# The last product of a fused attention and feed-forward kernel, its 128-row matmuls cut into two of 64 rows

## The chip, the core and the metric

The kernel runs on one NeuronCore of a Trainium2 chip. The metric is device time in microseconds (us) of one execution. TensorE multiplies: it holds a stationary block (the "weights" of one matmul) of up to 128 rows by 128 columns and streams a moving block of up to 512 columns past it; the sums over the rows go to PSUM, which has eight banks of 512 float32 for each of 128 partitions. VectorE (DVE) and ScalarE (ACT) empty the banks into SBUF, and DMA queues carry data between SBUF and the main memory. In profiles the loading of a stationary block stands on a row of its own, PEld.

## The reference

```python
attn = softmax(mask(q @ k.T / sqrt(64))) @ v          # 2 batches, 12 heads, 448 tokens, head size 64
x = attn as (896, 768)
h = max(x @ w1, x @ w2, x @ w3)                       # 768 -> 768
y = h @ w_out                                         # 768 -> 768
t = y @ w_in2                                         # 768 -> 2048
g = t if t > 0 else exp(t) - 1
out = g @ w_out2                                      # 2048 -> 768
```

The five weight matrices come as float64, everything else as float32.

## The kernel before

All products are computed transposed: a result block has 128 features on the partitions and the 448 tokens of one batch in the free dimension, so it fills most of one PSUM bank. The order of the program is attention (with some of the first product woven into it), then h, y, g and out, one block of 128 output features after another. In the code the results in PSUM are called `ph`, `py`, `pg` and `po`.

To keep float32 accuracy each operand is cut in two numbers of a shorter type (`F32R`): `hi` is the value rounded, `lo` the rest. A product needs three matmuls for each 128 rows of the contraction: hi by hi, hi by the rest of the activations, and lo by hi. `products` (lines 184 to 192) issues them for both batches: four matmuls with the weights `hi` (lines 189 and 190) and two with `lo` (line 192) for one chunk of 128 rows. Every matmul brings its own load of the 128x128 stationary block.

The weights are made by `weight_steps` (lines 144 to 178): a DMA brings float64 words, five DVE steps (lines 158 to 168) turn them into float32, ACT rounds them to `hi` (line 175), and DVE subtracts to get `lo` (line 142). The pool `wp` has two buffers for the raw words and for the float32, and three each for `hi` and `lo`, so this work runs ahead of TensorE by up to three blocks of weights.

The last product stands in lines 541 to 556: for each of the six blocks `f` of 128 output features the 16 chunks of the contraction come in three blocks of weights (6, 5 and 5 chunks), 96 matmuls for both batches together, 576 in all six. `psum` (line 486) gives the banks out in turn, all eight of them. After the 16 chunks DVE copies the bank of batch 0 and ACT that of batch 1 (line 555) into the tile `ot`, and SP's queue writes each to memory (line 556). In the last block of weights of the last `f` the batches are done one after the other, so that only batch 1 is left to copy and write at the very end.

In attention, the scores `s` (line 280) contract over a head size of 64: the two heads of a pair lie in the two row halves of TensorE and write to different banks. Their operands are plain float32; the chip runs such a matmul as two passes, and the profile shows each pass as an instruction of its own. Line 327 transposes `pr` into `pt` through the full array in one pass, and line 350 (`o`) uses all 128 rows and 64 columns.

Of the kernel before, what the change touches and what calls it, by code (L numbers as in the profile page):

```python
# [14 lines left out]
ALU = mybir.AluOpType  # L15
PSUM = bass.MemoryType.PSUM

B, H, S, D = 2, 12, 448, 64
# [7 lines left out]
NF = 2048 // 128  # L26
# [93 lines left out]
def fused_kernel(ctx: ExitStack, tc: tile.TileContext, qk, v, w1, w2, w3, wo, wi2, wo2, outT):  # L120
    nc = tc.nc
# [58 lines left out]
    def load_w(src, n, name):  # L180
        *_, parts = weight_steps(src, n, name)
        return parts

    def products(ps_list, hi, lo, xs_list, c0, n, total):

        for c in range(n):
            cc = c0 + c
            for ps, xs in zip(ps_list, xs_list):
                nc.tensor.matmul(ps, hi[:, c, :], xs[cc][:, 0, :], start=(cc == 0), stop=False)  # L189
                nc.tensor.matmul(ps, hi[:, c, :], xs[cc][:, 1, :], start=False, stop=False)  # L190
            for ps, xs in zip(ps_list, xs_list):
                nc.tensor.matmul(ps, lo[:, c, :], xs[cc][:, 0, :], start=False, stop=(cc == total - 1))  # L192

    x = [[None] * NK for _ in range(B)]
    y = [[None] * NK for _ in range(B)]

    with ExitStack() as s1:
# [13 lines left out]
        with ExitStack() as s2:  # L211
# [236 lines left out]
            def block(k, ready):  # L448

                f, n = AHEAD[k]  # L450
                u = {}

                def product(eng, c):
                    if c == 0:
                        u["ps"] = ps_m.tile([128, S], F32, tag="m", name=f"ph{n}_0_{f}")
                    hi, lo = ahead[f, n]
                    products([u["ps"]], hi[:, c:c + 1], lo[:, c:c + 1], [x[0]], c, 1, NK)

                def keep(eng):
                    if n == 0:  # L460
                        bests[f, 0] = bp.tile([128, S], F32, tag="best0", name=f"best0_{f}")
                    keep_best(bests[f, 0], u["ps"], n)

                t = ready
                for c in range(NK):
                    t = plan.add(product, (c,), {"PE": 610}, k if c == 0 else -20, [t, ready, xs_done[c if k == 0 else NK - 1]],
                        takes=["m"] * (c == 0), mode="x")
                return plan.add(keep, (), {"DVE" if n else "ACT": 540 if n else 420}, 0, [t], gives=["m"])
# [17 lines left out]
        def psum(name):  # L486
            pool, tag = banks[count[0] % 8]
            count[0] += 1
            return pool.tile([128, S], F32, tag=tag, name=name)

        h = [[None] * NK for _ in range(B)]
        for f in range(NK):
            best = [bests.get((f, b)) or bp.tile([128, S], F32, tag=f"best{b}", name=f"best{b}_{f}") for b in range(B)]
            for n, w in enumerate((w1, w2, w3)):
                over = range(1, B) if (f, n) in AHEAD else range(B)
                if (f, n) in AHEAD:
                    hi, lo = ahead[f, n]
                else:

                    with tc.issue_after(last["DVE"].ins):  # L500
                        hi, lo = load_w(w[f], NK, f"w{n}_{f}")
                ps = [psum(f"ph{n}_{b}_{f}") for b in over]
                products(ps, hi, lo, [x[b] for b in over], 0, NK, NK)
                for b in over:
                    keep_best(best[b], ps[b - over[0]], n)
            for b in range(B):
                hs = hp.tile([128, 2, S], F32R, tag="h", name=f"h{b}_{f}")
                nc.scalar.copy(hs[:, 0], best[b])
                sub(nc.vector, hs[:, 1], best[b], hs[:, 0])
                h[b][f] = hs  # L510
        for f in range(NK):
            hi, lo = load_w(wo[f], NK, f"wo_{f}")
            ps = [psum(f"py{b}_{f}") for b in range(B)]
            products(ps, hi, lo, h, 0, NK, NK)
            for b in range(B):
                ys = yp.tile([128, 2, S], F32R, tag="y", name=f"y{b}_{f}")
                nc.scalar.copy(ys[:, 0], ps[b])
                sub(nc.vector, ys[:, 1], ps[b], ys[:, 0])
                y[b][f] = ys
# [3 lines left out]
    g = [[None] * NF for _ in range(B)]  # L523
    for f in range(NF):
        hi, lo = load_w(wi2[f], NK, f"wi2_{f}")
        ps = [psum(f"pg{f}_{b}") for b in range(B)]
# [12 lines left out]
            sub(nc.vector, gs[:, 1], gf, gs[:, 0])  # L539
            g[b][f] = gs  # L540
    for f in range(NK):
        ps = [psum(f"po{f}_{b}") for b in range(B)]
        c0 = 0
        for n in (6, 5, 5):
            hi, lo = load_w(wo2[f, :, c0:c0 + n], n, f"wo2_{f}_{c0}")
            if f == NK - 1 and c0 + n == NF:
                for b in range(B):
                    products([ps[b]], hi, lo, [g[b]], c0, n, NF)
            else:
                products(ps, hi, lo, g, c0, n, NF)  # L550
            c0 += n
        for b in range(B):
            ot = ep.tile([128, S], F32, tag="ot", name=f"ot{f}_{b}")
            rows = outT[128 * f:128 * (f + 1), S * b:S * (b + 1)]
            (nc.scalar.copy if b else nc.vector.tensor_copy)(ot, ps[b])
            nc.sync.dma_start(rows, ot)


# [38 lines left out]
```

## Time and profile before

| | |
|---|---|
| median of 3 runs | 496.99 us (496.43 to 498.34) |
| span of the profiled execution, first to last instruction | 494.9 us |
| what the median has beyond that span | 2.1 us |
| TensorE matmul busy | 488.0 us, 99% of the span |
| TensorE weight loads busy | 425.2 us, 86% |
| VectorE, ScalarE busy | 374.7 us (76%), 183.4 us (37%) |
| the last product, first matmul to last | 374.5 to 491.0 us of the span |

The profile has no time of its own for the profiled execution beside its span. "Busy" counts the time in which at least one instruction of an engine is under way. Matmuls overlap: the duration of one is how long it takes to pass through, and the pace is the distance from one start to the next. "PEclk" is the granted TensorE clock as a share of 2.4 GHz. In a row of the timeline the first number is the start in us from the start of the span, the second the length in us of the (merged) instructions, then follow engine, line, operation, output<-inputs, shapes, and the count; in brackets stands how long the engine was idle ahead of it, and what ended that.

### The profile page before, as it was taken

To read this page: it belongs to the slowest core of one execution; us is meant where nothing else is said; L and a number is where in the kernel's file an instruction comes from. 1 tells how busy PE (TensorE), PEld (TensorE's weight loads), DVE (VectorE), ACT (ScalarE), POOL (GpSimd) and SP (SyncE) were. 2 spreads that over 40 slices of the span, in tenths; PEclk is the share of its full clock that TensorE was granted. 3 is DMA by queue.
4 is the path that set the end of the run, shared out by engine and by line. 5 is a ranking of instruction groups with operands and counts; after the bars stand their busy time and mean duration, and the time that the engine had idled before them with its cause. 6 is when DMAs were issued, how large, how long until landed. Compare 5 with 4: busy or idle time off the path is not lost.

```text
span 494.9 us, 6950 instructions
## 1 busy us (share of the span) xinstructions
PE 488.0 (99%) x2600; PEld 425.2 (86%) x2600; DVE 374.7 (76%) x719; ACT 183.4 (37%) x426; POOL 41.0 (8%) x95
## 2 busy tenths in 40 slices
PE   7999999999999999999999999999999999999997
PEld 3555757899999999999999999999999999999996
DVE  5999995599978778778778888988988756667310
ACT  6999795222202221221223654554553111111100
POOL 4475361000000000000000000000000000000000
PEclk9999999999999999999999999999999999999999
DMA  6635520045433332323332332332332444244010
GB/s 216 229 91 185 212 72 21 1 138 182 142 123 119 127 107 86 130 77 115 127 117 75 127 101 92 128 123 74 102 119 73 138 127 155 93 153 143 2 37 37
DMA packets 13969, 55.88 MB, mean 113 GB/s; under 512 B 1520, under 2 KB 3568, under 8 KB 13936
## 3 DMA queue, kind: packets, MB, share of 16 engines
q1 hardware_dynamic: 13936, 55.45, 33.3%
q8 instruction: 20, 0.33, 0.3%
q14 instruction: 13, 0.11, 0.1%
HBM read 52.69 MB, written 2.75 MB: 112 GB/s over the span
## 4 chain that ended last, share of the span: by engine, by line
PE 94%; DVE 3%; POOL 1%; DMA 1%; ACT 0%; issue 0%; SPq 0%; DVEq 0%; ACTq 0%
PE ph L189 9%; PE ph L192 9%; PE ph L190 9%; PE po L192 8%; PE pg L192 8%; PE po L190 8%; PE pg L190 8%; PE pg L189 8%; PE po L189 8%; PE pt L327 4%; PE o L350 4%; PE s L280 4%; PE py L192 3%; PE py L189 3%; PE py L190 3%; DVE pr L294 1%
## 5 line engine op out<-in xcount | busy, mean ns | idle before, releaser
L189 PE MATMUL ph<-x,hi_w 128*128 128x448 f32 x216 | 79.4, 368 | 0.0
L190 PE MATMUL ph<-x,hi_w 128*128 128x448 f32 x216 | 78.9, 365 | 0.0
L189 PE MATMUL po<-g,hi_wo 128*128 128x448 f32 x192 | 70.2, 366 | 0.0
L189 PE MATMUL pg<-y,hi_wi 128*128 128x448 f32 x192 | 70.2, 366 | 0.0
L190 PE MATMUL pg<-y,hi_wi 128*128 128x448 f32 x192 | 70.2, 365 | 0.0
L190 PE MATMUL po<-g,hi_wo 128*128 128x448 f32 x192 | 70.2, 365 | 0.0
L175 ACT CAST hi_wo<-f_wo 128x768 fp32r<-128x768 f32 (+1 forms) x24 | 18.8, 783 | 125.0 <-PE po L190 56.4
L192 PE MATMUL ph<-x,lo_w 128*128 128x448 f32 x216 | 64.3, 366 | 0.0
L192 PE MATMUL po<-g,lo_wo 128*128 128x448 f32 x192 | 55.4, 366 | 0.0
L192 PE MATMUL pg<-y,lo_wi 128*128 128x448 f32 x192 | 54.6, 365 | 0.0
L142 DVE TENSOR_TENSOR lo_wo<-f_wo,hi_wo 128x768 fp32r<-128x768 f32 (+1 forms) x24 | 21.4, 891 | 31.8 <-ACT hi_wo L175 31.8
L189 PEld LDWEIGHTS ph<-x,hi_w 128*128 128x128 f32 x216 | 40.6, 188 | 3.2
L192 PEld LDWEIGHTS ph<-x,lo_w 128*128 128x128 f32 x216 | 40.6, 188 | 3.2
L190 PEld LDWEIGHTS ph<-x,hi_w 128*128 128x128 f32 x216 | 40.6, 188 | 3.1
L175 ACT CAST hi_w<-f_w 128x768 fp32r<-128x768 f32 x18 | 15.1, 837 | 70.2 <-PE ph L190 45.5
L189 PEld LDWEIGHTS po<-g,hi_wo 128*128 128x128 f32 x192 | 36.1, 188 | 2.8
L189 PEld LDWEIGHTS pg<-y,hi_wi 128*128 128x128 f32 x192 | 36.1, 188 | 2.8
L192 PEld LDWEIGHTS po<-g,lo_wo 128*128 128x128 f32 x192 | 36.1, 188 | 2.8
L192 PEld LDWEIGHTS pg<-y,lo_wi 128*128 128x128 f32 x192 | 36.1, 188 | 2.8
L190 PEld LDWEIGHTS pg<-y,hi_wi 128*128 128x128 f32 x192 | 36.1, 188 | 2.8
L190 PEld LDWEIGHTS po<-g,hi_wo 128*128 128x128 f32 x192 | 36.1, 188 | 2.8
L304 ACT ACTIVATE pr<-pr,nmx 128x384 f32<-128x384 f32 (+1 forms) x72 | 35.9, 502 | 5.3 <-DVE nmx L294 5.3
(80 smaller groups left out, 804.6 us busy)
## 6 DMA issues: line engine op xcount, KB each, us to landing
raw_w<-in_w SPq DMA_DIRECT2D x18, 768.0 KB, 4.4
raw_wi<-in_wi SPq DMA_DIRECT2D x16, 768.0 KB, 4.3
raw_wo<-in_wo SPq DMA_DIRECT2D x12, 768.0 KB, 4.4
raw_wo<-in_wo SPq DMA_DIRECT2D x12, 640.0 KB, 4.0
qk<-in_qk SPq DMA_DIRECT2D x11, 448.0 KB, 4.7
v<-in_v SPq DMA_DIRECT2D x12, 256.0 KB, 3.5
out_t<-ot SPq DMA_DIRECT2D x12, 224.0 KB, 3.1
qk<-in_qk SPq DMA_DIRECT2D x1, 256.0 KB, 3.1
```

Source lines behind the costliest of these rows:

```text
L142: return eng.tensor_tensor(out=out, in0=a, in1=b.bitcast(F32), op=ALU.subtract)
L175: nc.scalar.copy(hi, fb)
L189: nc.tensor.matmul(ps, hi[:, c, :], xs[cc][:, 0, :], start=(cc == 0), stop=False)
L190: nc.tensor.matmul(ps, hi[:, c, :], xs[cc][:, 1, :], start=False, stop=False)
L192: nc.tensor.matmul(ps, lo[:, c, :], xs[cc][:, 0, :], start=False, stop=(cc == total - 1))
L280: nc.tensor.matmul(out, us[e]["qk"][own, 0, C * i:w], us[e]["qk"][own, 1, :w], start=True, stop=True, skip_group_check=True)
L294: nc.vector.tensor_tensor_reduce(out=pr, in0=u["s", g][j or 0][:, at:at + w], in1=mask_r if i == NB else mask[:, FULL - w:], scale=-0.125, ...
L304: nc.scalar.activation(pr, pr, AF.Exp, bias=u["nmx"][:, n:n + 1], scale=-1.0, accum_out=u["l"][:, n:n + 1])
L327: nc.tensor.transpose(pt[:e - C * c, at:at + C], u["pr", j if j is None else j ^ odd, i][:, C * c:e], ident)
L350: nc.tensor.matmul(u["o"][D * j:D * (j + 1), C * c:], u["v"][:, j, c], u["th_r"][:, j ^ odd] if c == NB else u["th"][:, c, j ^ odd, C * c: ...
```

## The change

Each matmul of the last product is cut into one over rows 0 to 63 and one over rows 64 to 127 of the same stationary and moving blocks. The two halves accumulate into banks of their own (so a block `f` holds four banks, not two), and alternate: lower half, upper half, for each of the three terms. When the sums are done, ACT copies the bank of the lower half into `ot`, and DVE adds the bank of the upper half to it, for both batches. Everything ahead of the last product is as it was.

```diff
+    def products_by_rows(pairs, hi, lo, xs_list, c0, n, total):
+
+        for c in range(n):
+            cc = c0 + c
+            for parts in (((hi, 0), (hi, 1)), ((lo, 0),)):
+                for pair, xs in zip(pairs, xs_list):
+                    for w, part in parts:
+                        for ps, at in zip(pair, (0, 64)):
+                            rows = slice(at, at + 64)
+                            nc.tensor.matmul(
+                                ps, w[rows, c, :], xs[cc][rows, part, :], start=cc == 0 and w is hi and part == 0,
+                                stop=cc == total - 1 and w is lo)
...
     for f in range(NK):
-        ps = [psum(f"po{f}_{b}") for b in range(B)]
+        ps = [[psum(f"po{f}_{b}_{r}") for r in range(2)] for b in range(B)]
         c0 = 0
         for n in (6, 5, 5):
             hi, lo = load_w(wo2[f, :, c0:c0 + n], n, f"wo2_{f}_{c0}")
             if f == NK - 1 and c0 + n == NF:
                 for b in range(B):
-                    products([ps[b]], hi, lo, [g[b]], c0, n, NF)
+                    products_by_rows([ps[b]], hi, lo, [g[b]], c0, n, NF)
             else:
-                products(ps, hi, lo, g, c0, n, NF)
+                products_by_rows(ps, hi, lo, g, c0, n, NF)
             c0 += n
         for b in range(B):
             ot = ep.tile([128, S], F32, tag="ot", name=f"ot{f}_{b}")
             rows = outT[128 * f:128 * (f + 1), S * b:S * (b + 1)]
-            (nc.scalar.copy if b else nc.vector.tensor_copy)(ot, ps[b])
+            nc.scalar.copy(ot, ps[b][0])
+            nc.vector.tensor_tensor(out=ot, in0=ps[b][1], in1=ot, op=ALU.add)
             nc.sync.dma_start(rows, ot)
```

On TensorE, at the start of the last product, the row of a matmul names output, moving and stationary block; `po_0` is batch 0 and `po_1` batch 1. Before:

```order
L189 MATMUL po_0_3635<-g_0_2634,hi_wo_0_0_3645 128x448
L190 MATMUL po_0_3635<-g_0_2634,hi_wo_0_0_3645 128x448
L189 MATMUL po_1_3636<-g_1_2642,hi_wo_0_0_3645 128x448
L190 MATMUL po_1_3636<-g_1_2642,hi_wo_0_0_3645 128x448
L192 MATMUL po_0_3635<-g_0_2634,lo_wo_0_0_3646 128x448
L192 MATMUL po_1_3636<-g_1_2642,lo_wo_0_0_3646 128x448
```

With the change, where `po_0_0` and `po_0_1` are the two row halves of batch 0:

```order
L203 MATMUL po_0_0_3635<-g_0_2634,hi_wo_0_0_3647 128x448
L203 MATMUL po_0_1_3636<-g_0_2634,hi_wo_0_0_3647 128x448
L203 MATMUL po_0_0_3635<-g_0_2634,hi_wo_0_0_3647 128x448
L203 MATMUL po_0_1_3636<-g_0_2634,hi_wo_0_0_3647 128x448
L203 MATMUL po_1_0_3637<-g_1_2642,hi_wo_0_0_3647 128x448
L203 MATMUL po_1_1_3638<-g_1_2642,hi_wo_0_0_3647 128x448
```

The order of the terms stays, and each matmul has become a pair; there are 1152 where there were 576.

On DVE, where the first block `f` ends, before:

```order
L168 SCALAR_TENSOR_TENSOR f_wo_2_0_3919<-raw_wo_2_0_3917,f_wo_2_0_3919 128x768
L555 COPY ot_0_3769<-po_0_3635 128x448
L142 TENSOR_TENSOR lo_wo_1_11_3876<-f_wo_1_11_3869,hi_wo_1_11_3875 128x640
L158 TENSOR_SCALAR f_wo_2_6_3967<-raw_wo_2_6_3965 128x640
L160 TENSOR_SCALAR f_wo_2_6_3967<-f_wo_2_6_3967 128x640
```

and with the change:

```order
L168 SCALAR_TENSOR_TENSOR f_wo_2_0_4121<-raw_wo_2_0_4119,f_wo_2_0_4121 128x768
L142 TENSOR_TENSOR lo_wo_1_11_4044<-f_wo_1_11_4037,hi_wo_1_11_4043 128x640
L569 TENSOR_TENSOR ot_0_3867<-po_0_1_3636,ot_0_3867 128x448
L569 TENSOR_TENSOR ot_1_3871<-po_1_1_3638,ot_1_3871 128x448
L158 TENSOR_SCALAR f_wo_2_6_4205<-raw_wo_2_6_4203 128x640
L160 TENSOR_SCALAR f_wo_2_6_4205<-f_wo_2_6_4205 128x640
```

One copy became two additions, and they stand behind the `lo` of the next block's weights rather than ahead of it.

## Rows read from the trace of the kernel before

**Rows 1.** The page: busy time, granted clock, and the chain that ended last
```profile
span 494.9 us, 6950 instructions
PE 488.0 (99%) x2600; PEld 425.2 (86%) x2600; DVE 374.7 (76%) x719; ACT 183.4 (37%) x426; POOL 41.0 (8%) x95
PEclk9999999999999999999999999999999999999999
PE 94%; DVE 3%; POOL 1%; DMA 1%; ACT 0%; issue 0%; SPq 0%; DVEq 0%; ACTq 0%
```

**Rows 2.** Windows over the six blocks of po: busy us (instructions), clock, DMA
```profile
394.00:413.00 19.00, 19.00 (x95) 17.64 (x94) 12.99 (x19) 2.48 (x4) 0.00 (x0) 1.00 0.42 135
...
sum 117.50, PE 116.91 PEld 108.13 DVE 65.22 ACT 17.58 POOL 0.00; mean PE 19.48 PEld 18.02 DVE 10.87 ACT 2.93 POOL 0.00
```

**Rows 3.** The tile po: ns min/median/max of one, first and last start
```profile
L189 PE MATMUL po<-g,hi_wo x192: 361/365/370, 374.5 to 490.6; 128*128 128x448 f32 x192
L192 PE MATMUL po<-g,lo_wo x192: 362/365/370, 375.3 to 491.0; 128*128 128x448 f32 x192
L555 DVE COPY ot<-po x6: 623/624/625, 394.0 to 488.4; 128x448 f32<-128x448 f32 x6
L555 ACT COPY ot<-po x6: 522/527/532, 394.4 to 491.5; 128x448 f32<-128x448 f32 x6
```

**Rows 4.** Timeline within po: matmuls, and the loads for the next ones
```profile
398.83 0.36 PE L189 MATMUL po<-g,hi_wo 128*128 128x448 f32 x1
398.83 0.19 PEld L190 LDWEIGHTS po<-g,hi_wo 128*128 128x128 f32 x1
399.03 0.36 PE L190 MATMUL po<-g,hi_wo 128*128 128x448 f32 x1
```

**Rows 5.** Timeline in attention: scores in the two row halves, two groups of passes
```profile
5.36 1.14 PE L280 MATMUL s<-qk 64*128 64x384 f32 x8 [0.52 <-DMA qk<-in_qk]
60.71 1.17 PEld L280 LDWEIGHTS s<-qk 64*128 64x128 f32 x12 [0.20 <-issue]
60.71 1.57 PE L280 MATMUL s<-qk 64*128 64x384 f32 x12
```

**Rows 6.** Chain that ended last: start us, us, transposes and scores
```profile
58.04 0.80 PE pt L327 x6
70.89 0.92 PE pt L327 x7
```

**Rows 7.** Timeline in attention: F32R matmuls, the last followed by a transpose
```profile
81.12 0.37 PE L190 MATMUL ph<-x,hi_w 128*128 128x448 f32 x1
81.33 0.37 PE L192 MATMUL ph<-x,lo_w 128*128 128x448 f32 x1
81.54 0.27 PE L327 MATMUL pt<-ident,pr 128*128 128x128 f32 x1
```

**Rows 8.** Groups by line and shape: x count, busy us, mean ns of one
```profile
L205 DVE TENSOR_TENSOR best<-ph,best 128x448 f32<-128x448 f32 x24 | 14.0, 619 | 18.9 <-PE ph L192 18.9
L350 PE MATMUL o<-th_r,v 128*64 128x64 f32 x48 | 3.4, 221 | 0.0
```

**Rows 9.** Timeline where the second block f begins, and after
```profile
393.76 0.73 ACT L175 CAST hi_wo<-f_wo 128x640 fp32r<-128x640 f32 x1 [5.35 <-PE po L190]
394.39 0.53 ACT L555 COPY ot<-po 128x448 f32<-128x448 f32 x1
395.38 0.49 DVE L158 TENSOR_SCALAR f_wo<-raw_wo 128x640 int32<-128x640 int32 x1
397.83 0.82 DVE L168 SCALAR_TENSOR_TENSOR f_wo<-raw_wo,f_wo 128x640 int32<-128x640 int32 x1
401.10 0.83 ACT L175 CAST hi_wo<-f_wo 128x768 fp32r<-128x768 f32 x1 [6.18 <-issue]
```

**Rows 10.** Timeline of the end, and four short passes of o
```profile
491.04 0.37 PE L192 MATMUL po<-g,lo_wo 128*128 128x448 f32 x1
491.49 0.53 ACT L555 COPY ot<-po 128x448 f32<-128x448 f32 x1 [18.70 <-PE po L192]
492.05 0.33 SPq L556 DMA_DIRECT2D out_t<-ot  x1
...
59.69 0.28 PE L350 MATMUL o<-th_r,v 128*64 128x64 f32 x4
```

## The prediction

> **What bounds the kernel now.** First the page: TensorE has a matmul under way for 99% of the span, the chain of waits that ended last runs over PE for 94% of it, and the granted clock is full (2.4 GHz) throughout [rows 1]. The reader is to see that only the pace of TensorE, and what stands behind its last matmul, can move the time. Second the windows over the last product, po: TensorE is busy for 116.9 of 117.5 us, DVE for 65.2, ACT for 17.6 [rows 2]. The other engines have room there. Third the pace, which busy time does not give, since matmuls overlap. The first of the 576 matmuls starts at 374.5, the last at 491.0 [rows 3]: 116.5 us over 575 steps is 202.6 ns a step, and single steps in the timeline agree (398.83 to 399.03) [rows 4]. Streaming 448 columns, one in each clock of 2.4 GHz, would take 186.7 ns. So **16 ns in each step are something else**, 9.2 us over the stage. The change is worth what it does to these 16 ns, and costs what it adds.
>
> **The row halves.** The change turns 576 steps into 576 pairs. How long is a pair? The scores in attention are the one place of the trace with two 64-row matmuls in two row halves and two banks. A group of 8 passes (two pairs 384 columns wide, two 128 wide) takes 1.14 us, one of 12 (two more pairs, 256 wide) 1.57 us [rows 5]. So 512 columns more, in both halves, cost 0.43 us. These are plain float32 passes, which take two clocks a column: a seventh transpose of 128 columns adds 0.12 us to six [rows 6], against 107 ns at two clocks. At that rate 512 columns are 427 ns, if the halves run side by side, and 853 ns if one waits for the other. **They run side by side**, loads included, and little is left over: 3 ns in two pairs, with 10 ns of rounding in each of the two rows, at most some 10 ns a pair.
>
> So do the 16 ns go with the halves? The rows allow two readings. Either they belong to changing the stationary block of the full array, and the scores are free of them since they run in halves; or they belong to a stream of the type F32R at one column a clock, and the scores are free of them since their streams run at half that rate. What tells the two apart is the transposes: full array, a new stationary block each, two clocks a column, and the seventh costs 0.11 to 0.12 us where 0.107 is the stream [rows 6]. The full array changes its block there for a few ns. And where an F32R matmul is followed by a transpose, whose load is short and done early, the step is still 0.21 us, as between two F32R matmuls before it (81.12, 81.33, 81.54) [rows 7]. So the 16 ns come with the F32R stream, whatever follows. Each half streams the same 448 columns of F32R at the same rate, beside the other, so I take the pair at today's step, 202.6 ns: **no change from the matmuls, 0.0 us**. The bounds, from these rows: below, a pair as free of extras as the scores, 186.7 + 3 = 189.7 ns, which is 576 x 12.9 ns = -7.4 us; above, two halves that wait for each other, 2 x 186.7 + 3 = 376 ns, +100 us. I take the middle because the transposes, the nearest row for the full array, speak against the first, and the scores against the last.
>
> The Trainium skill says in "TensorE: Matmul & The Clock Gate", Part 3, The mechanism, that a weight load overlaps a matmul in flight only where the row groups differ. By that rule the full array would pay for its loads now and the halves would not, and the sum would be the lower bound. Here the trace differs: in po the load of the next block starts with the running matmul of the full array, both at 398.83 [rows 4].
>
> The number of matmuls doubles: 1152 in 117 us is one in 101 ns. Four short passes of `o` fit in 0.28 us, where one alone takes 0.22 [rows 10, 8], so four start within 0.06 us. Handing out matmuls costs nothing here; if it could only keep 110 ns apart, it would cost 1152 x 9 ns = 10 us.
>
> **The change of tiling.** Going from the full array to halves idles the loads for 0.20 us in attention [rows 5], against nothing in an unbroken run. It happens once: **+0.2 us**.
>
> **Emptying the banks.** For each block f one DVE copy (624 ns) and one ACT copy (527) [rows 3] become two ACT copies and two DVE additions; the same form of addition, a bank and a tile, takes 619 ns in line 205 [rows 8]. Over six blocks ACT gets 3.2 us more and DVE 12 x 0.619 - 6 x 0.624 = 3.7 us more, against 52 us in which DVE is idle and 100 for ACT [rows 2]. The queues: ACT rounds weights until 394.49 and then copies, now twice, to about 395.5; DVE adds at 394.95 and 395.5, and the next block's first weight step, at 395.38 before [rows 9], starts near 396.1, 0.7 us later. Its last step then ends at 399.4 and not 398.65, still ahead of the rounding at 401.10, which waits for a free buffer [rows 9]. The `lo` of the next block now stands ahead of the additions and does not wait. Four banks a block leave the other four of eight to the next block, and they are needed again only 19 us later. Nothing of it reaches TensorE: **0.0 us**. If that cover were gone, each block would pay the 0.7 us, 4 us in all.
>
> **The end.** Now ACT starts the last copy at 491.49, 0.45 us after the start of the last matmul, and the write to memory follows at 492.05 [rows 10]. With the change an addition stands between them: 0.62 us and a hand-over of 0.03, as between that copy's end at 492.02 and the write. All of it is on the path: **+0.65 us**.
>
> **Sum.** 0.0 + 0.2 + 0.65 = +0.85 us. The profiled execution's span, 494.9, becomes 495.7; the median of the runs has 2.1 us more than that span, and I keep those: 496.99 + 0.85 = **497.8 us**. The uncertain part is the step: in one stretch of attention F32R steps take 0.206 to 0.207 us (81.12 to 81.54) [rows 7], 4 ns over po's, and I allow as much on the other side but somewhat less: 200 to 206.5 ns is -1.5 to +2.2 us, so this case has the range 496 to 500.
>
> **The rivals.**
> *The 16 ns vanish in the halves.* The block change of the full array is then what costs, by a mechanism that spares transposes. For it: every F32R matmul of the trace runs in the full array, and every float32 matmul that is no transpose runs in halves or on half the columns, so no row shows F32R in halves. Against it: the transposes and the step of rows 7. Time: 497.8 - 7.4 = 490.4 us. Chance 0.31.
>
> *The pair is longer than the step,* since the second half starts after the first and the next pair waits for both. What the rows leave open is up to some 7 ns a pair [rows 5]; 576 x 7 = 4.0 us, 501.8 us. It decides from 205.4 ns a pair on, where 0.85 + 576 x 2.8 ns reaches 2.5 us. For it: all those steps would pay it, and nothing covers it. Against it: the 512 columns that cost 0.43 us. Chance 0.17.
>
> The Trainium skill's page "TensorE: Matmul & The Clock Gate", Part 3, Measured speedup vs the span model, gives about 4 ns for each further tile. That speaks against this change, and would make an estimated 576 x 4 = 2.3 us of this rival. No row here resolves it.
>
> *The halves do not run side by side in F32R,* so that the change does not do what it says. The scores deliver a sum in each half every two clocks, one a clock for both; F32R would deliver two a clock down the same columns into two banks, and no row shows that rate on all 128 columns. If one a clock is the limit, a pair takes 376 ns and the kernel 497.8 + 100 = 598 us. Chance 0.08.
>
> **How the numbers follow.** My own case has 0.44. About 0.5% (2.5 us) is what a measurement of this kernel can tell from no change. Faster than that needs a pair under 196.8 ns, which the first rival brings: 0.31. Slower needs one over 205.4 ns: the second and third rival, 0.25, and of my own case the top end, 0.02, makes 0.27. Same: 0.42. The range is to leave out at most 0.2: from below the first rival's 490.4, with a ns a pair to spare, to above the second's 501.8, leaving out the third and some of the second's tail: 489.8 to 503.0.
>
> **What would show it.** In the profile after, first and last start of po's matmuls give the pair: 116.7 us between them means 202.6 ns and this forecast, 109 us the first rival, 121 the second, 216 the third. The two matmuls of a pair should start within 10 ns of each other. The last matmul should be followed by an ACT copy, an addition of 0.62 us and the write; TensorE should not idle where a block f begins, and DVE's weight steps should come 0.7 us later there. A stage of another length at an unchanged pair, or an idle TensorE, would make the prediction wrong in its sum as well as in its reason.

## The result, and the profile after

| | before | after |
|---|---|---|
| first comparison | 497.06 us, 4 runs (496.43 to 498.34) | 501.11 us, 4 runs (500.46 to 501.76) |
| ratio, 95% interval | | 1.0077 [1.0060, 1.0095] |
| the same kernel again, on another occasion | 497.03 us, 12 runs (496.73 to 504.93) | 499.96 us, 6 runs (497.99 to 500.72) |
| ratio, 95% interval | | 1.0049 [1.0032, 1.0066] |
| span of the profiled execution, first comparison | 494.9 us | 498.7 us (its own time 500.46) |

The change makes the kernel slower, by 0.8% in the first comparison and by 0.5% in the second: beyond the 0.5% that I called measurable, and at its edge. Its ten executions do not lie around one value: eight lie between 499.8 and 501.8, two at 498.0 and 498.1. The experiments show two lengths of one step on TensorE behind this, both at full granted clock; the text calls them the short and the long step.

The page of the kernel after, its busy times, its chain and its costliest group:

```profile
span 498.7 us, 8124 instructions
PE 490.9 (98%) x3176; PEld 424.9 (85%) x3176; DVE 377.6 (76%) x725; ACT 186.2 (37%) x432; POOL 41.0 (8%) x95
...
PE 95%; DVE 3%; POOL 1%; ACT 0%; issue 0%; DVEq 0%
...
L203 PE MATMUL po<-g,hi_wo 64*128 64x448 f32 x768 | 95.8, 365 | 0.0
```

576 more matmuls, DVE and ACT each 3 us busier, the chain on PE as in [rows 1], and no idle time in front of the new matmuls. The page says that TensorE is the bound, as before, and not that its pace has changed. That is read from starts. The tile po of the kernel after (ns min/median/max of one, first and last start in us):

```profile
L203 PE MATMUL po<-g,hi_wo x768: 359/365/472, 375.3 to 494.0; 64*128 64x448 f32 x192
...
L203 PE MATMUL po<-g,lo_wo x384: 363/365/365, 376.2 to 494.2; 64*128 64x448 f32 x192
...
L568 ACT COPY ot<-po x12: 525/532/539, 395.7 to 494.6; 128x448 f32<-128x448 f32 x12
L569 DVE TENSOR_TENSOR ot<-po,ot x12: 612/616/624, 396.5 to 495.2; 128x448 f32<-128x448 f32 x12
```

From 375.3 to 494.2 us it is 118.9 us for 576 pairs, where [rows 3] had 116.5. Behind the first pair every step is 206 or 207 ns, 206.67 on average. Before, the average was 202.67: single steps went from 198 to 208 ns there, in a run that repeats every six matmuls (203, 199, 207, 202, 203, 202), so that one step of 207 ns tells nothing and the mean over six or more does. The steps of this text are such means. The difference is 574 x 4.0 ns = 2.3 us. The ends of po, in the timeline after:

```profile
374.58 0.37 PE L190 MATMUL pg<-y,hi_wi 128*128 128x448 f32 x1
374.79 0.57 PE L192 MATMUL pg<-y,lo_wi 128*128 128x448 f32 x2
375.29 1.09 PE L203 MATMUL po<-g,hi_wo 64*128 64x448 f32 x8
...
494.22 0.37 PE L203 MATMUL po<-g,lo_wo 64*128 64x448 f32 x2
494.62 0.53 ACT L568 COPY ot<-po 128x448 f32<-128x448 f32 x1 [2.56 <-PE po L203]
495.19 0.62 DVE L569 TENSOR_TENSOR ot<-po,ot 128x448 f32<-128x448 f32 x1 [2.47 <-ACT ot L568]
495.84 0.33 SPq L570 DMA_DIRECT2D out_t<-ot  x1
```

The last full-array matmul starts at 374.99 and the first pair at 375.29, 0.10 us more than a step; the second pair comes 0.31 us later, another 0.10. At the end the addition stands between copy and write, and from the last matmul's start to the end of the span it is 4.43 us where it was 3.83 [rows 1], [rows 10]. The rest of the difference, 0.68 us, was there before any F32R matmul ran (the first started at 53.93 and not at 53.26), in code that the change doesn't touch; over the profiled executions of all kernels here that start moves between 53.3 and 55.4 us. So 2.3 + 0.1 + 0.1 + 0.6 + 0.68 = 3.8 us, the difference of the spans.

### The profile page after: what moved, and what is told of

Read it like the earlier page. It is cut to its first block, busy times and chain, and to the rows that moved or that the text cites. A ratio compares the mean times of both kernels' runs of the same rounds, so it can differ in the third digit from the quotient of the medians.

```text
span 498.7 us, 8124 instructions
## 1 busy us (share of the span) xinstructions
PE 490.9 (98%) x3176; PEld 424.9 (85%) x3176; DVE 377.6 (76%) x725; ACT 186.2 (37%) x432; POOL 41.0 (8%) x95
## 4 chain that ended last, share of the span: by engine, by line
PE 95%; DVE 3%; POOL 1%; ACT 0%; issue 0%; DVEq 0%
PE po L203 24%; PE ph L189 9%; PE ph L192 9%; PE ph L190 9%; PE pg L192 8%; PE pg L190 8%; PE pg L189 8%; PE pt L340 4%; PE o L363 4%; PE s L293 4%; PE py L192 3%; PE py L190 3%; PE py L189 3%; DVE pr L307 2%; POOL pr L330 1%; PE idle L244 1%
## 5 line engine op out<-in xcount | busy, mean ns | idle before, releaser
L203 PE MATMUL po<-g,hi_wo 64*128 64x448 f32 x768 | 95.8, 365 | 0.0
L203 PEld LDWEIGHTS po<-g,hi_wo 64*128 64x128 f32 x768 | 71.9, 184 | 7.7 <-issue 0.3
L203 PE MATMUL po<-g,lo_wo 64*128 64x448 f32 x384 | 56.0, 365 | 0.0
L203 PEld LDWEIGHTS po<-g,lo_wo 64*128 64x128 f32 x384 | 35.9, 184 | 3.7
L175 ACT CAST hi_wi<-f_wi 128x768 fp32r<-128x768 f32 x16 | 13.4, 836 | 60.9 <-PE pg L190 44.1
L307 DVE CUSTOM_DVE_ANT_0 pr<-s,mask 128x384 f32<-128x384 f32 (+1 forms) x72 | 26.6, 413 | 7.0 <-PE s L293 6.9
```

The costliest lines, as they stand in the source:

```text
L175: nc.scalar.copy(hi, fb)
L203: nc.tensor.matmul(ps, w[rows, c, :], xs[cc][rows, part, :], start=cc == 0 and w is hi and part == 0, stop=cc == total - 1 and w is lo)
L307: nc.vector.tensor_tensor_reduce(out=pr, in0=u["s", g][j or 0][:, at:at + w], in1=mask_r if i == NB else mask[:, FULL - w:], scale=-0.125, ...
```

## The experiments

The expectations name theories. A: the second matmul of a pair comes some nanoseconds after the first and lengthens each pair. B: the 64-row F32R shape itself has the long step. C, put up after the first four runs: a chain of F32R matmuls of 448 columns has one of two steps, 202.67 or 206.67 ns, settled where the chain begins. D: 64 rows always have the long one.

**Half alone.** The change with its upper half left out: one 64-row matmul where there was a pair.

```diff
-                        for ps, at in zip(pair, (0, 64)):
+                        for ps, at in zip(pair, (0,)):
```

> The upper row half is left out of the last product (so half of each sum is missing): 576 matmuls of 64 rows, one bank for each result, ACT copies it out. Theory A (the second matmul of a pair adds its own 3 to 4 ns to the step): alone, a 64-row matmul has the step of the full array, 202.7 ns, 116.5 us from the first start to the last. Theory B (the shape costs it: an F32R matmul of 64 rows has a longer step): 206.7 ns, 118.8 us, as in the pairs. If the 16 ns beyond the stream belonged to the height of the array: under 197 ns.

```profile
L203 PE MATMUL po<-g,hi_wo x384: 365/365/466, 375.6 to 494.3; 64*128 64x448 f32 x192
...
L203 PE MATMUL po<-g,lo_wo x192: 363/365/365, 376.5 to 494.5; 64*128 64x448 f32 x192
```

500.52 us. In the tile po (`hi` and `lo`) the same 118.9 us, the same 206.67 ns a step, with no second half. Theory A falls: the second half costs nothing. By the Trainium skill, "TensorE: Matmul & The Clock Gate", Part 3, Measured speedup vs the span model, each further tile adds about 4 ns to the span of one group. The first result would have fitted that in size as a term of each step; as such this run doesn't bear it out, since the 4 ns stay when the further tile goes, and what agrees is the 3 to 4 ns between the starts of the two halves in the first measurement.

**Quarters.** Four matmuls of 32 rows, four banks, three additions.

```diff
-                        for ps, at in zip(pair, (0, 64)):
-                            rows = slice(at, at + 64)
+                        for ps, at in zip(pair, (0, 32, 64, 96)):
+                            rows = slice(at, at + 32)
```

> Four matmuls of 32 rows in place of two of 64, four banks for each result, three additions. Steps are counted by groups of four. Theory A: each further matmul adds 4 ns, 202.7 + 3 x 4 = 214.7 ns a group within a block f. Theory B: the shape sets the step, 206.7 ns or another value, with no term for the number of tiles. Both: at each of the six blocks TensorE waits for banks, since all eight are taken, some 3 to 5 us each, which is not in the step.

539.26 us. The step of A for four tiles doesn't appear. In undisturbed stretches each quarter runs as a chain of its own, at 202.7 or 206.7 ns, and two quarters can have different steps at the same time (over 3 us from 418 on, three go at 202.4 to 202.7 ns and one at 206.6). Most of the loss is elsewhere: a block now takes all eight banks, and TensorE waits until ACT's copies free them. That wait over po (us in total, times, longest), and windows of 5 us over the matmuls (us busy, count, granted clock, DMA share, GB/s):

```profile
PE po L203 <- ACT ot L568: 4.4, 5, 0.9
...
425.00:430.00 5.00, 4.71 (x88) 1.00 0.26 64
430.00:435.00 5.00, 4.40 (x27) 0.77 0.47 180
435.00:440.00 5.00, 5.00 (x64) 0.55 0.30 61
440.00:445.00 5.00, 5.00 (x105) 1.00 0.33 132
```

Where a block begins, 27 matmuls are counted in place of 105; the granted clock, full before that wait, falls, and over the next 5 us it is 0.55, near the lower level of 1.2 GHz. Six such heads are the loss of 32 us in po (151.0 us long), 5.3 us each where 3 to 5 had been expected, far more than any step. In this execution all products behind attention, in the full array and with code that the change doesn't touch, ran at 206.67 ns too: from the first of them to po it is 286.63 us (94.21 to 380.83), where the first measurement has 281.09 (94.20 to 375.29); the 5.54 us between them are 1386 steps of 4.0 ns. So the long step isn't the halves' own.

**Full array, two banks.** The kernel before, its even and odd chunks in two banks, emptied as in the change.

```diff
+                nc.tensor.matmul(pair[cc % 2], hi[:, c, :], xs[cc][:, 0, :], start=(cc < 2), stop=False)
...
-            (nc.scalar.copy if b else nc.vector.tensor_copy)(ot, ps[b])
+            nc.scalar.copy(ot, ps[b][0])
+            nc.vector.tensor_tensor(out=ot, in0=ps[b][1], in1=ot, op=ALU.add)
```

> Matmuls of the full array, but even and odd chunks of the contraction go to banks of their own, which ACT copies and DVE adds as in the changed kernel: the emptying alone, without row halves. Both theories: step 202.7 ns as before, no idle TensorE where a block begins, 0.65 us more behind the last matmul, so 497.7 us beside 497.0, same within the noise. If the emptying delays weights or banks: more than 499 us, with idle TensorE in po.

The ratio, between the executions near 497 us of both kernels, is 1.0001 [0.9983, 1.0019]; po in the profiled run takes 116.5 us at 202.67 ns, and no step where a block f begins is longer than within one: there the emptying is hidden. Behind the last matmul the 0.65 us that were expected did not come: from its start to the end of the span it is 3.94 us, 0.11 more than before, since the last chunk goes to one bank alone and ACT's copy of the other (492.95) starts before the last matmul (493.16). So this run tests the emptying within po, and not the end of the change. On this occasion both kernels, the one **before** too, had executions near 505 us as well (seven of 14 before, six of ten here). The distance, 8 us, is the number of all F32R matmuls times the same 4 ns: 2016 x 4.0 ns = 8.1 us. That is reckoned and not shown, as none of these executions was profiled; the quarters' trace shows the 5.5 us of it that lie between attention and po.

**Halves in turn.** The change with its loops exchanged: for `hi` two matmuls of the lower half, then two of the upper; for `lo` one of each, as before.

```diff
-                    for w, part in parts:
-                        for ps, at in zip(pair, (0, 64)):
+                    for ps, at in zip(pair, (0, 64)):
+                        for w, part in parts:
```

> As the changed kernel, but the halves do not alternate from one matmul to the next: for hi, both terms of the lower half, then both of the upper half. Theory A: a matmul waits for the one ahead of it in its own half only after others were handed out; two in the same half in a row make the next two wait, and at most one of two overlaps: about 1.5 steps a pair, 300 ns, po 175 us and 555 us in all; if matmuls start strictly in order and a half can hold no second one waiting, up to 405 ns for pairs that do not overlap. Theory B: 206.7 ns a pair if each half has a queue of its own.

500.84 us. The 555 us that theory A gave here did not come. The halves run beside each other as two chains. In the first third their distance drifts up and down between 5 and some 200 ns, by 4 ns a pair, as it must where one goes at 202.7 and the other at 206.7 ns; in the last two thirds both go at 206.7 and start 100 and 107 ns apart. po takes 118.9 us.

**The change again,** unaltered.

> The changed kernel unaltered, to see how its executions spread beside those of the kernel before, which came at about 497 and about 505 us in the last comparison (2016 F32R matmuls x 4.0 ns = 8.1 us between them). Theory C (an unbroken chain of F32R matmuls has one of two steps, 202.7 or 206.7 ns, settled where the chain begins, whatever its shape; the change breaks the chain where po begins): times at up to four places, 497.8 (all short), 500.1 (po alone long), 503.6 (po alone short) and 505.9 us (all long). Theory D (64 rows in F32R have the long step by their shape, always): two places alone, 500.1 and 505.9 us.

Four executions at 499.8 to 500.7 us, two at 498.0 and 498.1; the profiled one is one of the two. Its tile po:

```profile
L203 PE MATMUL po<-g,hi_wo x768: 355/362/468, 375.1 to 491.6; 64*128 64x448 f32 x192
...
L203 PE MATMUL po<-g,lo_wo x384: 358/362/366, 376.1 to 491.8; 64*128 64x448 f32 x192
```

116.6 us: 202.67 ns in both halves, the step of the full array, and the time is that of the forecast, 497.99 us beside 497.8. D and B fall, and A once more: these are pairs, and the second half of each, 10 ns behind the first here, adds nothing to the step. Over the same window in the first block, the two executions of one kernel can be set side by side (window and its length; busy us and count of PE, PEld, DVE and ACT, of tile po alone; clock, DMA share, GB/s). The first measurement:

```profile
376.00:392.00 16.00, 16.00 (x158) 14.50 (x156) 0.00 (x0) 0.00 (x0) 1.00 0.43 131
```

and this one:

```profile
376.00:392.00 16.00, 16.00 (x162) 15.34 (x160) 0.00 (x0) 0.00 (x0) 1.00 0.39 128
```

Busy all the time, clock 1.00 in both, 158 against 162 matmuls. Neither busy share nor clock shows the long step; only starts and counts do.

**Full array with breaks.** The kernel before, and one small matmul of 64 rows and 64 columns where each block f begins, which the real first matmul overwrites.

```diff
+            if c0 == 0:
+                nc.tensor.matmul(ps[0][:, :64], hi[:64, 0, :], g[0][0][:64, 0, :64], start=True, stop=True)
```

> The kernel before with one short 64-row matmul at the start of each of the six blocks f (its result is overwritten): the array changes to halves and back, six breaks, each costing 0.3 to 0.4 us, 2 us in all; the product itself stays in the full array. Theory C: some blocks go on at 206.7 ns though they are 128 rows high (all six: 2.3 us more, about 501.3 us; none: 499). Theory D: all six at 202.7 ns.

501.5 us, ratio 1.0095 [1.0078, 1.0112], from six matmuls. The timeline, in the first block and in the second:

```profile
392.49 0.36 PE L189 MATMUL po<-g,hi_wo 128*128 128x448 f32 x1
392.69 0.36 PE L190 MATMUL po<-g,hi_wo 128*128 128x448 f32 x1
...
393.70 0.36 PE L189 MATMUL po<-g,hi_wo 128*128 128x448 f32 x1
...
395.01 0.29 PE L547 MATMUL po<-g,hi_wo 64*128 64x64 f32 x1
...
404.02 0.37 PE L189 MATMUL po<-g,hi_wo 128*128 128x448 f32 x1
404.23 0.37 PE L190 MATMUL po<-g,hi_wo 128*128 128x448 f32 x1
...
405.26 0.37 PE L189 MATMUL po<-g,hi_wo 128*128 128x448 f32 x1
```

Six steps take 1.21 us in the first block (392.49 to 393.70; 1.216 in the trace's nanoseconds) and 1.24 in the second (404.02 to 405.26), and 1.24 in all later ones: 202.67 and 206.67 ns in the **full array**, in one execution. The rows of the stationary block do not decide; the step can change at a break of the chain (one of the six did it). The gap at a break itself is 0.52 us from the last matmul of a block to the first of the next.

**Halves nudged** and **full array nudged.** Does it take an idle moment at the break? Each block f gets one more matmul of another width, of the same tiling as its neighbours, so that nothing goes idle. In the halves a pair of 440, 256, 104, 72, 428 and 36 columns:

```diff
+            if c0 == 0:
+                w = (440, 256, 104, 72, 428, 36)[f]
```

> The changed kernel with one extra pair of matmuls at the start of each block f, 440, 256, 104, 72, 428 and 36 columns wide (overwritten later), so that each block's chain starts at another phase; together 0.8 us longer. Theory C: the step differs between the blocks, some at 202.7 ns, and can differ between the two halves. Theory D: 206.7 ns in all six.

and in the full array, from the second block on, 440, 256, 104, 72 and 428:

```diff
+            if c0 == 0 and f:
+                w = (0, 440, 256, 104, 72, 428)[f]
+                nc.tensor.matmul(ps[0][:, :w], hi[:, 0, :], g[0][0][:, 0, :w], start=True, stop=True)
```

> The kernel before with one extra matmul of the full array at the start of the blocks f = 1 to 5, 440, 256, 104, 72 and 428 columns wide (overwritten later): no change of tiling, nothing idle, only the phase moves; 0.6 us longer. Theory C with the phase alone as what decides: some of the five blocks go over to 206.7 ns. If only an idle or a change of tiling can settle the step anew: 202.7 ns throughout (or 206.7 throughout, if the execution began so).

499.16 and 498.02 us. In both, every block settles at 202.67 ns but the one behind the 428 columns, which settles at 206.67: the fifth block in the halves, the sixth in the full array. The timeline of the full array there:

```profile
472.00 0.37 PE L190 MATMUL po<-g,hi_wo 128*128 128x448 f32 x1
472.21 0.57 PE L192 MATMUL po<-g,lo_wo 128*128 128x448 f32 x2
472.61 0.36 PE L548 MATMUL po<-g,hi_wo 128*128 128x428 f32 x1
472.81 0.36 PE L189 MATMUL po<-g,hi_wo 128*128 128x448 f32 x1
...
484.16 0.37 PE L190 MATMUL po<-g,hi_wo 128*128 128x448 f32 x1
484.37 0.37 PE L189 MATMUL po<-g,hi_wo 128*128 128x448 f32 x1
484.58 0.37 PE L190 MATMUL po<-g,hi_wo 128*128 128x448 f32 x1
```

No idle time, no change of tiling, one matmul 20 columns narrower than its neighbours, and after a few steps the rest of the kernel goes at 206.67 ns (484.16, 484.37, 484.58). One of 440 columns, at the head of the second block, does not do it:

```profile
393.85 0.57 PE L192 MATMUL po<-g,lo_wo 128*128 128x448 f32 x2
394.26 0.36 PE L548 MATMUL po<-g,hi_wo 128*128 128x440 f32 x1
394.45 0.36 PE L189 MATMUL po<-g,hi_wo 128*128 128x448 f32 x1
```

That it is the moment at which the chain goes on is not shown: in the trace's nanoseconds the next matmul starts 195 ns behind the inserted one and 397 ns behind the last of 448 columns in both cases, and yet one goes on with the short step and the other with the long. A rival that no run tests is the width itself. In the two runs together the step changes three times in eleven: behind 428 columns in both, and behind the 36 in the halves, where it goes back to the short one. These are the widths that are no multiple of eight; behind 440, 256, 104 and 72 the step stays. The width can't be all of it either, since the change, one program, comes out with either step. What settles the step stays open. Where one chain runs, or two start side by side, it holds until a break or a matmul of another width; the halves in turn went over without either. The change brings in one such break, the change of tiling where po begins.

**One width per block,** in F32R and in bfloat16. The blocks of po are streamed 512, 480, 416, 384, 320 and 256 columns wide.

```diff
+        wide = (512, 480, 416, 384, 320, 256)[f]
...
+                        nc.tensor.matmul(
+                            ps[:, :n_cols], m[:, c, :], a[:, at:at + n_cols], start=first,
+                            stop=cc == total - 1 and m is lo, skip_group_check=True)
```

> The kernel before with matmuls of another width in each block f of the last product: 512, 480, 416, 384, 320 and 256 columns for 448 (so its sums are others). It measures what the step has beyond the stream of N columns at 2.4 GHz. If a fixed term for each matmul: N/2.4 + 16 ns (229, 216, 189, 176, 149, 123 ns), or + 20 ns in the long step. If it grows with the columns (8.6%): 232, 217, 188, 174, 145, 116 ns. If the step comes in whole units of 6.67 ns (206.67 is 31 of them, the short step is 30.4 on average): values that are not N/2.4 plus one constant.

> The same widths, with the weights and activations of the last product in bfloat16 (so its sums are others, and coarser), full array, a load for each matmul. The prediction put the 16 ns down to the stream of the type F32R. If so: N/2.4 + 3 ns, as the transposes have: 216, 203, 176, 163, 136, 110 ns. If they belong to changing the stationary block of the full array: the steps of the F32R kernel of this pair, 229 to 123 ns.

Two rows of each timeline, six steps apart, in the block of 512 columns. F32R:

```profile
379.95 1.07 PE L205 MATMUL po<-g,hi_wo 128*128 128x512 f32 x4
...
381.31 1.07 PE L205 MATMUL po<-g,hi_wo 128*128 128x512 f32 x4
```

and bfloat16:

```profile
379.91 1.03 PE L205 MATMUL po<-g,hi_wo 128*128 128x512 bf16 x4
...
381.21 1.03 PE L205 MATMUL po<-g,hi_wo 128*128 128x512 bf16 x4
```

1.36 and 1.30 us. (The whole runs, 483.17 and 476.66 us, stream fewer columns, and their times say nothing by themselves.) The settled steps, and what they have beyond one column in each clock of 2.4 GHz:

| columns | 512 | 480 | 448 (other runs) | 416 | 384 | 320 | 256 |
|---|---|---|---|---|---|---|---|
| F32R, ns | 226.7 | 216.7 | 202.7 or 206.7 | 188.3 | 173.3 | 146.7 | 120.0 |
| beyond the columns | 13.3 | 16.7 | 16.0 or 20.0 | 15.0 | 13.3 | 13.3 | 13.3 |
| bfloat16, ns | 215.8 | 202.5 | | 175.8 | 162.5 | 135.8 | 109.2 |
| beyond the columns | 2.5 | 2.5 | | 2.5 | 2.5 | 2.5 | 2.5 |

In F32R none of the three forms that were named fits all widths. In units of 6.67 ns the steps are 34, 32.5, 30.4 or 31, 28.25, 26, 22 and 18: whole at four widths and in the long step of 448, where the single steps are alike to about 1 ns, and not whole at 480, 416 and in the short step of 448, where they repeat an uneven run.

In bfloat16, with a new full-array block for each matmul as well, 2.5 ns are left, as forecast. The 16 ns come with F32R and not with changing the full array's block. One thing changed beside the stream: a load takes 98 ns in bfloat16 and 188 in F32R. That the longer load is not what costs is argued from two rows: at 256 columns the F32R step, 120.0 ns, is shorter than its load, and in [rows 7] the step is as long ahead of a transpose, whose load takes 141 ns. No run streams F32R without a load for each matmul.

**Pieces of 512 and 384 columns** for the products behind attention (but for blocks begun within it), in place of two of 448, to escape the two steps of 448.

```diff
+    EVEN, WIDE, T = ((0, S), (S, 2 * S)), ((0, 512), (512, 2 * S)), 2 * S
...
+            for ps, (a, z) in zip(ps_list, cuts):
+                nc.tensor.matmul(ps[:, :z - a], hi[:, c, :], xs[cc][:, 0, a:z], start=(cc == 0), stop=False)
```

> All products after attention take the 896 tokens of both batches as a piece of 512 and a piece of 384 columns, in place of two of 448, full array, as before the change; what is computed is the reference's. Theory C (the length of a step in this stream depends on the width, and only 448 has two lengths): matmuls of 512 and of 384 columns alternate by half passes at 226.7 and 173.3 ns, together 400.0 ns for what two of 448 take in 405.3; over about 954 such pairs that is 5.1 us less, so about 492 us beside a kernel before of 497, and beside executions of the kernel before at 505 as well: no execution of this kernel at the longer time. Rival: the 13.3 ns beyond the columns' own time that the widths of 512 and 384 showed don't hold here (a chain that changes its width, or one that begins at another moment, has a longer step there too); a pair then takes 405 ns or more, and the time is 497 or above. A third outcome is that the unlike pieces make TensorE wait at their boundaries (a piece of 384 columns leaves less time to empty the banks), which the idle time of TensorE ahead of the products would show.

504.55 us (five runs, 504.0 to 504.7), ratio 1.0152 [1.0138, 1.0165]: a miss, and the rival's case. No idle time stands ahead of these matmuls; the steps are long:

```profile
299.75 0.40 PE L189 MATMUL pg<-y,hi_wi 128*128 128x512 f32 x1
299.98 0.40 PE L190 MATMUL pg<-y,hi_wi 128*128 128x512 f32 x1
300.22 0.34 PE L189 MATMUL pg<-y,hi_wi 128*128 128x384 f32 x1
300.40 0.34 PE L190 MATMUL pg<-y,hi_wi 128*128 128x384 f32 x1
300.57 0.58 PE L192 MATMUL pg<-y,lo_wi 128*128 128x512 f32 x2
300.99 0.40 PE L189 MATMUL pg<-y,hi_wi 128*128 128x512 f32 x1
```

Six steps take 1.24 us (299.75 to 300.99), a mean of 206.67 ns, the long step of 448 columns once more: 20 ns beyond the columns, where either width by itself has 13.3.

**Pieces in turn.** The same pieces, but with the loops exchanged: 15 to 18 matmuls of one width, then as many of the other.

```diff
-        for c in range(n):
-            cc = c0 + c
-            for ps, (a, z) in zip(ps_list, cuts):
+        for ps, (a, z) in zip(ps_list, cuts):
+            for c in range(n):
+                cc = c0 + c
```

> The pieces of 512 and 384 columns of the run before, but each load of weights is taken through for all blocks of the 512 piece first and then for the 384 piece, so that 15 to 18 matmuls of one width follow each other before the width changes; what is computed is the reference's. Theory C, amended (a width has its settled step only where matmuls of that width follow each other, as in the run of one width per block; where widths alternate every one to three matmuls, as in the run before, the long addition of 20 ns stays): after a few steps at each change the steps are 226.7 and 173.3 ns, mean near 200.0; up to 5.1 us off the 497 of the kernel before, less what some 100 changes of width cost at up to some 20 ns each, so 492 to 494 us. Rival 1: the long addition belongs to 512 or 384 in a chain that began at this moment, whatever follows; the steps stay at 233 to 238 and 175 to 180, and the time is about 504.5 again. Rival 2: the weights are needed sooner (a piece wants all blocks of a load within half the time), and TensorE waits for them at the heads of the pieces: then the steps are short, and the time is lost in gaps with DVE or ACT as the releaser.

495.37 us (12 runs, 495.0 to 497.4), ratio 0.9969 [0.9955, 0.9984]. The timeline over the head of a piece of 512:

```profile
301.13 0.39 PE L189 MATMUL pg<-y,hi_wi 128*128 128x512 f32 x1
301.36 0.40 PE L190 MATMUL pg<-y,hi_wi 128*128 128x512 f32 x1
301.59 0.40 PE L191 MATMUL pg<-y,lo_wi 128*128 128x512 f32 x1
301.83 0.39 PE L189 MATMUL pg<-y,hi_wi 128*128 128x512 f32 x1
...
303.89 0.39 PE L189 MATMUL pg<-y,hi_wi 128*128 128x512 f32 x1
...
304.57 0.39 PE L189 MATMUL pg<-y,hi_wi 128*128 128x512 f32 x1
```

The first nine steps of a piece of 512 are 224 to 236 ns, then they settle: three steps take 0.70 us from 301.13 and 0.68 from 303.89. Over 17 steps the mean is 229.1 ns in a piece of 512 columns, and 174.9 in one of 384. Against the settled 226.7 and 173.3 that is 17 x 2.4 + 17 x 1.6 = 68 ns at the two changes of width. So 36 matmuls take 7.27 us where 36 steps of 202.67 take 7.30. The gain of 5.1 us that the settled steps would bring is mostly given back at the changes: 1.5 us is left, and the time is above the 492 to 494 us that were expected. It is the one version here that computes the same and is faster than both kernels, if by little.

## Why the prediction was right or wrong

The time lay inside the range of 489.8 to 503.0, but the likeliest case, no change at 497.8 us, is not what the first measurement showed; the rival nearest to it in time, 501.8 us, named a mechanism that did not happen. The range reached up to 503.0 for that rival's sake, so that it holds the 501.11 us is in part luck.

- **"I take the pair at today's step, 202.6 ns"** is the term that was off, in its size and not in its comparison. Right in it: a pair costs what a matmul of the full array costs. The halves start side by side, 3 to 4 ns apart with the long step and 10 with the short one, and one half alone takes as long as both. Wrong: that the stream has one step. It has two, and behind the change of tiling it came out long in the first profiled execution and short in the second; the long one is 574 x 4.0 = 2.3 us. By their times eight of ten executions have it, though only one of the eight was profiled. With it the sum gives 497.8 + 2.3 = 500.1 us, where those eight lie at 499.8 to 501.8.
- **The row was there.** [Rows 7] had steps of 0.206 to 0.207 us in the kernel before. The prediction took them for an uncertainty about the mean and put 4 ns at the upper end of its own case, +2.2 us and 500 us, with a chance of 0.02 for more than 2.5. Two steps can't tell, as the short step has single ones of 207 ns; but the trace has 13 in a row there, 78.85 to 81.54, with a mean of 206.6. They were a second value, exact and lasting, and should have been a case of their own.
- **"The 16 ns come with the F32R stream, whatever follows"** was right, and with it the first rival deserved less than its 0.31: bfloat16 with a load for each matmul has 2.5 ns, F32R 13.3 to 20.0, and no half is faster than the full array. But "16 ns" is no constant of the stream, it depends on the width and on the beginning of the chain.
- **The second rival,** a pair that waits for its second half, was right about the sign and size (206.67 is above the 205.4 ns from which it was to decide) and wrong about the cause: the half alone has the same step. Its time alone would have settled on the wrong story. For what its rows leave open the prediction has some 10 ns a pair in one place and 7 in another; 3 ns and 10 of rounding over two pairs are 6.5.
- **The third rival** did not happen: both halves deliver at full rate.
- **The change of tiling, +0.2 us,** was right: 0.10 us ahead of the first pair and 0.10 behind it. What it does to the chain behind it was not seen.
- **Emptying the banks, 0.0 us,** was right: no step of po behind the first pair is longer than 207 ns, not even where a block f begins, and the ratio is 1.0001 with the emptying alone. Line 158, which began at 395.38 [rows 9], now begins at 397.59; 1.26 us of that is the block ending later, so it moved by 0.95 and not by 0.7: the first addition stands behind `lo` and starts only as that ends, at 396.52. TensorE doesn't wait for it.
- **The end, +0.65 us,** was right: 0.60, with the order copy, addition, write as forecast.

## What to carry to other kernels

Cutting a contraction that fills all 128 rows into row halves gained nothing here: both halves stream the same columns as the whole, and an addition and twice the banks come on top. Where one engine is busy all the time, read its pace from starts or counts in equal windows, and if a dozen steps in a row have another mean than the rest, take it as a second state with a cause and not as scatter. In the F32R streams of this kernel, long stretches of one width were the fastest, and a break of the chain could bring in the longer step.

## What the runs showed that was not expected

- Two lasting steps of the same F32R stream at 448 columns, 202.67 and 206.67 ns, at full granted clock: 2.3 us over po, 5.5 us over the products between attention and po, by count 8 us over all. It can change at a break of the chain, or behind one matmul 20 columns narrower. Why it comes out as the one or the other stays open; no run looked inside a step.
- 13.3 ns beyond the columns at 512, 384, 320 and 256 columns in long stretches of one width, but 20.0 ns on average where 512 and 384 alternate every one or two matmuls. After a change of width it takes up to nine steps to settle (230, 233, 236, 224, 231, 236, 228, 232 and 231 ns at 512, then 227).
- Four matmuls of 32 rows run as four chains, each with its own step: three at 202.4 to 202.7 ns beside one at 206.6.
